# A fused FFT-mixing and ReGLU kernel: fold pieces over 26 steps, one fifth value product in 12 steps, transform work over 33 steps, tail stores per group

## Chip, cores, metric

One core of one Trainium2 chip. The metric is the device time of one execution in microseconds.

Names: PE is TensorE's matmuls, PEld its weight loads, DVE is VectorE, ACT ScalarE, POOL GpSimd, SP SyncE (which issues most transfers). An engine name with a q (SPq, ACTq, POOLq) is its sequencer, where transfers are issued.

## The reference, cut to what matters

```python
# x: (8, 3008, 256) f32; w_gate, w_val: (256, 1536); w_out: (1536, 256)
X = np.fft.fft(np.fft.fft(x, axis=1), axis=2).real      # "mixing"
gate = np.maximum(X @ w_gate, 0.0)
val  = X @ w_val
out  = gate * val @ w_out                               # (24064, 256) f32
```

## The kernel before

The sequence of 3008 is split as 94 x 32. GpSimd *folds* a batch (adds mirrored columns of x, so that half a transform is enough), TensorE runs two transform stages, and the transform along the last axis is folded into the weights. The main loop has 288 *steps*: 8 batches x 3 blocks x 12 slices `f` of the hidden width. One step makes the products for 512 rows and also for their 512 mirror rows, and it runs a twelfth of the output product of the block before. The work of the next batches (load, fold, transform) is placed at fixed steps by `plan`.

```python
# a piece of a fold; the main loop takes one piece (one yield) per step
XC = 3
def fold(b, eng):                       # eng is GpSimd
    for lo in range(1, J - 1, XC):      # XC columns at a time: 5 x 3 pieces, 2 for the ends
        ...                                                         # eo <- xl, xh (small)
        yield eng.tensor_tensor(x1[:, :, 1:D], x1[:, :, 1:D], free(xh[0:NA], ...), op=ALU.add)
        for op, o in ((ALU.add, 1), (ALU.subtract, H + 1)):
            yield eng.tensor_tensor(e1[:, :, o:o + H - 1], x1[:, :, 1:H], free(x1, ...), op=op)

def split(t):                           # which steps do without the fifth value product
    return 18 <= t < len(steps) and t % 6 != 5

# gate:  G = wc.p0 + ws.p1 -> relu -> gs  (ScalarE);  then G += wm.p1 -> relu -> gm (mirror rows)
# value: V = wc.p0, then (split) E = even part of V (VectorE), then V += ws.p1
def value(t, part):
    ...
        nc.vector.tensor_tensor(e["h"][:, 0, :], e["gs"][:], e["V"][:], op=ALU.mult)

def mirror_value(t):
    if split(t):                        # mirror value = 2*even - V on VectorE, product on GpSimd
        nc.vector.scalar_tensor_tensor(e["E"][:, cols], e["E"][:, cols], 2.0, e["V"][:, cols],
                                       op0=ALU.mult, op1=ALU.subtract)
        mirror_h(t, nc.gpsimd, e["E"])
    else:                               # unsplit: a fifth value product on TensorE, product on VectorE
        nc.tensor.matmul(e["V"][:, cols], lhsT=wm[1][...], rhs=pqt[b, blk][:, 1, cols], ...)
        mirror_h(t, nc.vector, e["V"])

# gm and E have four buffers, V three, G two (PSUM banks)

def out_piece(t, half):                 # 4 of the 96 output matmuls of a block
    ...                                 # po: one PSUM tile (one bank) for two row groups s
    if s % 2 == 1 and ff == NF - 1:
        nc.scalar.copy(os_[:, s - 1:s + 1, :], po[:])
    if s == 3 and ff == NF - 1:
        store(b, blk, sg, os_)          # four DMAs of 128 KB on SyncE's queue

# steps of load, fold, stage 1, shuffle, rotation, stage 2 of the next batches, from the batch's start
plan = {0: (18, 24, (18, 19, ...), 26, 32, (33, 34, ...)),
        1: (7, 13, range(6, 14), 14, 22, (23, 25, 27, 29, 31, 33))}
```

In an *unsplit* step TensorE does one matmul more, but VectorE does one pass less and GpSimd does no mirror product.

Of the kernel before, what the change touches and what calls it, by code (L numbers as in the profile page):

```python
# [11 lines left out]
F32 = mybir.dt.float32  # L12
# [4 lines left out]
SB = bass.MemoryType.SB  # L17
# [5 lines left out]
def view(ap, offset, dims):  # L23

    return bass.AP(ap.tensor, ap.offset + offset, [list(d) for d in dims])


def free(ap, offset, *dims):

    part = list(ap.ap[0])  # L30
    return bass.AP(ap.tensor, ap.offset + offset, [part] + [list(d) for d in dims])
# [12 lines left out]
def kernel(ctx: ExitStack, tc, x, w_gate, w_val, w_out, out):  # L44
# [3 lines left out]
    nc = tc.nc  # L48
    B, S, D = x.shape
    DF = w_gate.shape[1]  # L50
    NA, NB = 94, 32
    H = D // 2
    NF = DF // 128
    NKA = 12
    NBLK = 3
    J = NB // 2 + 1

    const = ctx.enter_context(tc.tile_pool(name="const", bufs=1, space=SB))
    xp = ctx.enter_context(tc.tile_pool(name="xp", bufs=1, space=SB))
    tp = ctx.enter_context(tc.tile_pool(name="tp", bufs=2, space=SB))  # L60
    hp = ctx.enter_context(tc.tile_pool(name="hp", bufs=2 * NF + 1, space=SB))
    psd = ctx.enter_context(tc.tile_pool(name="psd", bufs=1, space=PS))
    psg = ctx.enter_context(tc.tile_pool(name="psg", bufs=2, space=PS))
    psv = ctx.enter_context(tc.tile_pool(name="psv", bufs=3, space=PS))
# [11 lines left out]
    XC = 3  # L76

    def load_x(b, q):
        xl = xp.tile([96, J, D], F32, tag="xl", name="xl")
        xh = xp.tile([96, NB // 2, D], F32, tag="xh", name="xh")  # L80
        for p0, n in ((0, 80), (80, 14)):
            q.dma_start(out=xl[p0:p0 + n],
                        in_=view(x, b * S * D + p0 * NB * D, [[NB * D, n], [1, J * D]]))

        nc.gpsimd.indirect_dma_start(out=xh[:].rearrange("p j d -> p (j d)"), out_offset=None,
                                     in_=view(x, 0, [[NB * D // 2, 2 * B * NA], [1, NB * D // 2]]),
                                     in_offset=bass.IndirectOffsetOnAxis(ap=ix[:, b:b + 1], axis=0))
        xt[b] = (xl, xh, tp.tile([NA, J, D], BF16, tag="eo", name="eo"))

    def fold(b, eng):  # L90


        xl, xh, eo = xt[b]
        for lo in range(1, J - 1, XC):
            n = min(XC, J - 1 - lo)
            x1, e1, m = xl[0:NA, lo:lo + n, :], eo[:, lo:lo + n, :], (NB // 2 - lo) * D
            eng.tensor_tensor(free(e1, 0, [D, n], [H, 2]), free(x1, 0, [D, n], [H, 2]),
                              free(xh[0:NA], m, [-D, n], [H, 2]), op=ALU.add)
            yield eng.tensor_tensor(x1[:, :, 1:D], x1[:, :, 1:D], free(xh[0:NA], m + D - 1, [-D, n], [-1, D - 1]),  # L99
                                    op=ALU.add)  # L100
            for op, o in ((ALU.add, 1), (ALU.subtract, H + 1)):
                yield eng.tensor_tensor(e1[:, :, o:o + H - 1], x1[:, :, 1:H], free(x1, D - 1, [D, n], [-1, H - 1]),  # L102
                                        op=op)
        ends = free(xl[0:NA], 0, [(J - 1) * D, 2], [H, 2])
        eng.tensor_copy(free(eo[:], 0, [(J - 1) * D, 2], [H, 2]), ends)
        for op, o in ((ALU.add, 1), (ALU.subtract, H + 1)):
            yield eng.tensor_tensor(
                free(eo[:], o, [(J - 1) * D, 2], [1, H - 1]), free(xl[0:NA], 1, [(J - 1) * D, 2], [1, H - 1]),
                free(xl[0:NA], D - 1, [(J - 1) * D, 2], [-1, H - 1]), op=op)
# [172 lines left out]
    with tc.tile_pool(name="sp", bufs=1, space=SB) as sp:  # L282
# [124 lines left out]
        for cs, off in enumerate((o0, o1)):  # L407
# [4 lines left out]
            t2 = sp.tile([128, 4, NB], F32, tag=f"m2t{cs}")  # L412
# [26 lines left out]
        for _ in fold(1, pl):  # L439
            pass  # L440
# [9 lines left out]
    ep = ctx.enter_context(tc.tile_pool(name="ep", bufs=4, space=SB))  # L450
    op = ctx.enter_context(tc.tile_pool(name="op", bufs=2, space=SB))

    steps = [(b, blk, f) for b in range(B) for blk in range(NBLK) for f in range(NF)]
    ht = {}

    def mirrored(t):

        blk = steps[t][1]
        return slice(NB if blk == 0 else 0, 512 - NB if blk == NBLK - 1 else 512)

    def split(t):

        return 18 <= t < len(steps) and t % 6 != 5

    def gate(t):
        b, blk, f = steps[t]
# [21 lines left out]
    def value(t, part):  # L488
        b, blk, f = steps[t]
        e, pq, fs = ht[t], pqt[b, blk], slice(f * 128, (f + 1) * 128)  # L490
        if part == 0:
            e["V"] = psv.tile([128, 512], F32, tag="v", name="V")
            nc.tensor.matmul(e["V"][:], lhsT=wc[1][:, fs], rhs=pq[:, 0, :], start=True, stop=split(t))  # L493
        else:
            nc.tensor.matmul(e["V"][:], lhsT=ws[1][:, fs], rhs=pq[:, 1, :], start=False, stop=True,  # L495
                             skip_group_check=split(t))
            nc.vector.tensor_tensor(e["h"][:, 0, :], e["gs"][:], e["V"][:], op=ALU.mult)  # L497
# [8 lines left out]
    def mirror_h(t, eng, val):  # L506

        e, cols = ht[t], mirrored(t)
        eng.tensor_tensor(free(e["h"][:], 512 + cols.start + NB - 1, [NB, (cols.stop - cols.start) // NB], [-1, NB]),  # L509
                          e["gm"][:, cols].rearrange("p (a k) -> p a k", k=NB),  # L510
                          val[:, cols].rearrange("p (a k) -> p a k", k=NB), op=ALU.mult)

    def mirror_value(t):
        b, blk, f = steps[t]
        e, cols = ht[t], mirrored(t)
        if split(t):
# [3 lines that stand above are left out]
        else:  # L520
            nc.tensor.matmul(e["V"][:, cols], lhsT=wm[1][:, f * 128:(f + 1) * 128], rhs=pqt[b, blk][:, 1, cols],  # L521
                             start=False, stop=True, skip_group_check=True)
            mirror_h(t, nc.vector, e["V"])

    state = {}

    def out_piece(t, half):

        b, blk, f = steps[t]
        for k in range(8 * f + 4 * half, 8 * f + 4 * half + 4):  # L530
            gi, ff = divmod(k, NF)
            sg, s = divmod(gi, 4)
            g = 3 - s if sg else s
            if s == 0 and ff == 0:
                state["os"] = op.tile([128, 4, D], F32, tag="os", name="os")
            if s % 2 == 0 and ff == 0:
                state["po"] = pso.tile([128, 2, D], F32, tag="o", name="po")
            po, os_ = state["po"], state["os"]
            nc.tensor.matmul(po[:, s % 2, :], lhsT=ht[t - f + ff]["h"][:, sg, g * 128:(g + 1) * 128],  # L539
                             rhs=wo[:, ff, :], start=(ff == 0), stop=(ff == NF - 1))  # L540
            if s % 2 == 1 and ff == NF - 1:
                nc.scalar.copy(os_[:, s - 1:s + 1, :], po[:])  # L542
            if s == 3 and ff == NF - 1:
                store(b, blk, sg, os_)

    def store(b, blk, sg, os_):
        for u in range(4):
            ka = NKA * u + 4 * blk
            src = os_[32 * u:32 * u + 32].rearrange("p g d -> p (g d)")
            if sg == 0:  # L550
                nc.sync.dma_start(out=view(out, (b * S + ka) * D, [[NA * D, NB], [1, 4 * D]]), in_=src)
                continue

            lo = 1 if ka + 3 == 47 else 0
            hi = 3 if ka == 0 else 4
            row = b * S + NA - ka - 3 + lo
            nc.sync.dma_start(out=view(out, row * D, [[NA * D, NB], [1, (hi - lo) * D]]),
                              in_=src[:, lo * D:hi * D])
# [3 lines left out]
    def at(t, fn, *args):  # L562
        extra.setdefault(t, []).append(lambda: fn(*args))

    at(0, fold_w, 1, 1, 1, "dve")
    for k in range(4):
# [3 lines left out]


    plan = {0: (18, 24, (18, 19, 20, 21, 22, 23, 24, 25), 26, 32, (33, 34, 35, 37, 39, 41)),
            1: (7, 13, range(6, 14), 14, 22, (23, 25, 27, 29, 31, 33))}
    for b in range(B):
        t0 = b * NBLK * NF
        tl, tf, t1, tsh, tr, t2 = plan[min(b, 1)]
        if b + 2 < B:
            at(t0 + tl, load_x, b + 2, nc.sync)
            at(t0 + tf, lambda b=b: folds.append(fold(b + 2, nc.gpsimd)))
        if b + 1 < B:  # L580
            for c, k in zip((1, 2, 3, 4, 5, 6, 7, 0), t1):
                at(t0 + k, stage1, b + 1, c, "act")
            at(t0 + tsh, shuffle_out, b + 1, 0, 8)
            at(t0 + tsh, shuffle_in, b + 1, 0, NKA)
            at(t0 + tr, rotate, b + 1)
            for i, k in enumerate(t2):
                at(t0 + k, stage2, b + 1, i // 2, i % 2, "act")

    folds = []
    n = len(steps)  # L590
# [56 lines left out]
```

## Time and profile before

Median 662.8 us of 3 runs when the prediction was made. The profiled execution spans 660.6 us.

| | before |
|---|---|
| PE busy | 637.0 us (96%) |
| DVE / POOL / ACT busy | 553.3 (84%) / 468.8 (71%) / 426.7 (65%) us |
| 512-column matmuls, start to start (median) | 0.216 us |
| 256-column output matmuls, start to start (median) | 0.109 us |
| stalls of PE from step 48 on (below) | 12.7 us |
| last matmul to the end | 4.9 us |

From the page, part 1 (busy us, share of the span, number of instructions) and the first line of part 4 (the chain of work that ended last, by engine):

```profile
span 660.6 us, 12759 instructions
PE 637.0 (96%) x4266; PEld 410.1 (62%) x4266; DVE 553.3 (84%) x871; ACT 426.7 (65%) x809; POOL 468.8 (71%) x630
...
PE 81%; POOL 11%; DVE 5%; issue 2%; ACT 1%; POOLq 0%; DVEq 0%
```

TensorE is the limit almost all of the time. The 11% of GpSimd in the chain is the interesting part, since GpSimd is busy only 71% of the span.

How far a busy TensorE is from its best can be measured from the starts of its matmuls. The Trainium skill ("TensorE: Matmul & The Clock Gate", Back-to-back issue gap) gives columns/2.4 + 2.5 ns for an isolated matmul (what it says of streams is taken up in the last section), which is 215.8 ns for 512 and 109.2 ns for 256 columns; the trace's medians, 216 and 109 ns, agree. I therefore took the mirrored gate product (the trace has its record in all 288 steps), measured from one to the next, and subtracted the sum of this formula over the matmuls that the built program has between them (one small matmul of 12 columns per batch is counted as 25 ns; the traces show 29). Where nothing waits, the difference is within 6 ns of zero. The rest I call *stalls*. From step 48 to 287 the kernel has 490.7 us of matmuls and 12.7 us of stalls. They cluster in the folds: the steps from 60 to 71, for example, have 1.77 us of them, 1.13 us of it in one step, and the twelve after them 0.09 us.

GpSimd inside a fold (timeline: start us, duration us, engine, line, operation, out<-in):

```profile
162.48 0.24 POOL L97 TENSOR_TENSOR eo<-xl,xh 94x6 bf16<-94x6 f32 x1
162.79 1.81 POOL L99 TENSOR_TENSOR xl<-xl,xh 94x765 f32<-94x765 f32 x1
164.56 1.27 POOL L509 TENSOR_TENSOR h<-gm,E 128x512 bf16<-128x512 f32 x1
165.80 0.99 POOL L102 TENSOR_TENSOR eo<-xl 94x381 bf16<-94x381 f32 x1
166.74 1.27 POOL L509 TENSOR_TENSOR h<-gm,E 128x512 bf16<-128x512 f32 x1
167.98 0.99 POOL L102 TENSOR_TENSOR eo<-xl 94x381 bf16<-94x381 f32 x1
168.93 1.26 POOL L509 TENSOR_TENSOR h<-gm,E 128x512 bf16<-128x512 f32 x1
170.15 0.22 POOL L97 TENSOR_TENSOR eo<-xl,xh 94x6 bf16<-94x6 f32 x1
```

Three mirror products (L509, one per split step) and one group of three columns (L97, L99, twice L102) take 170.15 - 162.48 = 7.67 us without a gap. Three split steps of TensorE take 3 x 1.95 = 5.86 us. So during a fold GpSimd is slower than TensorE, whatever its share of the whole span. How this reaches TensorE is in the chain (start us, us, what), read from the bottom up:

```profile
156.36 1.81 POOL xl L99
158.16 1.24 POOL h L509
159.40 0.02 issue
159.42 0.02 ACT gm L486
159.45 0.47 issue
159.92 0.60 ACT gs L473
...
160.56 0.38 PE G L483
```

The mirrored gate product L483 adds into a bank that a ScalarE relu (L473) must read first, and waited for it; that relu stood behind the relu into gm (L486), which waited for a gm buffer, and the buffer was still needed by a mirror product (L509) that stood behind a 1.81 us fold piece (L99). The view of waits (engine, line, waited for: us in total, times, longest) sums these up: `ACT gm L486 <- POOL h L509: 27.4, 32, 1.4`.

```profile
ACT gm L486 <- POOL h L509: 27.4, 32, 1.4
...
DVE E L503 <- POOL h L509: 3.3, 11, 0.4
```

ScalarE's waits for PE, left out here, are healthy (it waits for work). These two lines are GpSimd holding up the engines ahead of it. What of it reaches TensorE, in the same view for TensorE alone:

```profile
PE G L483 <- ACT gs L473: 7.7, 8, 1.1
...
PE V L495 <- DVE E L503: 0.5, 3, 0.2
```

(This view covers the whole run and leaves out short waits.) Start to start and from step 48 on, 6.9 us of the 12.7 us of stalls, in 11 steps, stand before the mirrored gate product, which waits for ScalarE; 5.8 us, in 39 steps, stand before the second value product, which waits for VectorE's pass that computes E. The tail, in the timeline (a bracket gives the idle time before and what ended it):

```profile
653.16 0.58 ACT L542 COPY os<-po 128x512 f32<-128x512 f32 x1 [2.08 <-PE po L539]
655.73 0.58 ACT L542 COPY os<-po 128x512 f32<-128x512 f32 x1 [1.99 <-PE po L539]
656.34 1.72 SPq L557 DMA_DIRECT2D out_dram<-os  x4
```

After the last matmul (655.7 us) come a copy, four issues that take 1.72 us and 2.5 us until the end.

### The profile page before, as it was taken

The numbers are of one execution on the slowest core, as the hardware profiler recorded it, in microseconds if no ns is written. First come the engines' busy times: TensorE is split into PE (matmuls) and PEld (weight loads), VectorE is DVE, ScalarE is ACT, GpSimd is POOL, SyncE is SP. The second block draws the span as 40 slices with busy tenths as digits, with TensorE's granted clock in tenths as the row PEclk, the third lists the DMA queues.
The fourth block names the chain that finished last, engine by engine and source line by source line (L and its number), as shares of the span: only waits on it lengthen the run. The fifth ranks groups of instructions, "written<-read, shape, count | busy, mean of one in ns | idle before, by whom it ended". The sixth has DMA issues, their size and how long they took to land.

```text
span 660.6 us, 12759 instructions
## 1 busy us (share of the span) xinstructions
PE 637.0 (96%) x4266; PEld 410.1 (62%) x4266; DVE 553.3 (84%) x871; ACT 426.7 (65%) x809; POOL 468.8 (71%) x630
## 2 busy tenths in 40 slices
PE   6789999999999999999999999999999999999997
PEld 3424666665666666666666666666656666666665
DVE  9857688888788887989888887988979898899991
ACT  5465676775667766676676766676666766666662
POOL 9639579959975599658995599756996355455451
PEclk9799999999999999999999999999999999999999
DMA  9792472393126721196114922177111241211113
GB/s 252 239 202 51 127 202 78 85 234 104 42 78 142 192 82 49 41 196 190 40 53 106 226 81 69 51 161 221 41 42 49 67 118 39 81 33 43 51 32 94
DMA packets 32294, 70.76 MB, mean 107 GB/s; under 512 B 4475, under 2 KB 21491, under 8 KB 30227
## 3 DMA queue, kind: packets, MB, share of 16 engines
q1 hardware_dynamic: 29892, 58.16, 32.3%
q0 software_dynamic: 2336, 11.80, 9.0%
q8 instruction: 33, 0.54, 0.3%
q14 instruction: 33, 0.26, 0.1%
HBM read 39.77 MB, written 30.96 MB: 107 GB/s over the span
## 4 chain that ended last, share of the span: by engine, by line
PE 81%; POOL 11%; DVE 5%; issue 2%; ACT 1%; POOLq 0%; DVEq 0%
PE po L539 33%; PE V L495 9%; PE V L493 8%; PE G L472 8%; PE G L471 8%; PE G L483 8%; POOL h L509 3%; POOL eo L102 3%; POOL xl L99 2%; PE V L521 2%; PE ps L162 2%; POOL eo L130 2%; DVE E L503 1%; PE psw L261 1%; PE ps L204 1%
## 5 line engine op out<-in xcount | busy, mean ns | idle before, releaser
L509 POOL TENSOR_TENSOR h<-gm,E 128x480 bf16<-128x480 f32 (+1 forms) x225 | 276.0, 1227 | 147.5 <-DVE E L517 128.2
L539 PE MATMUL po<-wo,h 128*128 128x256 bf16 x2304 | 333.5, 272 | 0.0
L539 PEld LDWEIGHTS <-h 128*128 128x128 bf16 x2304 | 222.7, 98 | 88.2 <-issue 3.9
L486 ACT ACTIVATE gm<-G 128x480 f32<-128x480 f32 (+1 forms) x288 | 167.3, 581 | 141.8 <-PE G L483 112.1
L497 DVE TENSOR_TENSOR h<-gs,V 128x512 bf16<-128x512 f32 x288 | 193.9, 686 | 32.6 <-PE V L495 22.0
L503 DVE SCALAR_TENSOR_TENSOR E<-nb,af,V 128x480 f32<-128x480 bf16 (+1 forms) x225 | 163.0, 724 | 16.4 <-PE V L493 10.5
L473 ACT ACTIVATE gs<-G 128x512 f32<-128x512 f32 x288 | 171.5, 595 | 0.8 <-PE G L472 0.8
L517 DVE SCALAR_TENSOR_TENSOR E<-E,V 128x480 f32<-128x480 f32 (+1 forms) x225 | 148.1, 658 | 0.0
L483 PE MATMUL G<-pq,wm 128*128 128x480 bf16 (+1 forms) x288 | 106.6, 370 | 7.8 <-ACT gs L473 7.7
L495 PE MATMUL V<-pq,ws 128*128 128x512 bf16 x288 | 109.0, 378 | 1.1 <-DVE E L503 0.5
L472 PE MATMUL G<-pq,ws 128*128 128x512 bf16 x288 | 109.1, 379 | 0.4 <-DVE pq L209 0.4
L471 PE MATMUL G<-pq,wc 128*128 128x512 bf16 x288 | 109.1, 379 | 0.0
L493 PE MATMUL V<-pq,wc 128*128 128x512 bf16 x288 | 109.1, 379 | 0.0
L542 ACT COPY os<-po 128x512 f32<-128x512 f32 x96 | 56.2, 586 | 58.4 <-PE po L539 58.4
L509 DVE TENSOR_TENSOR h<-gm,V 128x480 bf16<-128x480 f32 (+1 forms) x63 | 41.9, 665 | 39.3 <-ACT gm L486 33.8
L102 POOL TENSOR_TENSOR eo<-xl 94x381 bf16<-94x381 f32 x70 | 69.0, 992 | 0.4
L99 POOL TENSOR_TENSOR xl<-xl,xh 94x765 f32<-94x765 f32 x35 | 63.2, 1806 | 2.7
L495 PEld LDWEIGHTS <-ws 128*128 128x128 bf16 x288 | 28.1, 98 | 33.9
L472 PEld LDWEIGHTS <-ws 128*128 128x128 bf16 x288 | 28.1, 98 | 31.5 <-issue 0.2
L172 ACT CAST t<-ps 96x512 bf16<-96x512 f32 x63 | 36.9, 585 | 6.6 <-PE ps L160 5.4
L493 PEld LDWEIGHTS <-wc 128*128 128x128 bf16 x288 | 28.1, 98 | 14.8 <-issue 7.0
L471 PEld LDWEIGHTS <-wc 128*128 128x128 bf16 x288 | 28.1, 98 | 13.1 <-issue 9.7
(106 smaller groups left out, 346.0 us busy)
## 6 DMA issues: line engine op xcount, KB each, us to landing
out_dram<-os SPq DMA_DIRECT2D x176, 128.0 KB
xl<-in_x_dram SPq DMA_DIRECT2D x7, 1360.0 KB
Td<-t SPq DMA_DIRECT2D x7, 768.0 KB
t<-Td SPq DMA_DIRECT2D x7, 768.0 KB
nb<-Nd SPq DMA_DIRECT2D x24, 128.0 KB
xl<-in_x_dram SPq DMA_DIRECT2D x7, 238.0 KB
xl<-in_x_dram SPq DMA_DIRECT2D x4, 384.0 KB
xh<-in_x_dram SPq DMA_DIRECT2D x4, 384.0 KB
```

The source lines that it names most:

```text
L471: nc.tensor.matmul(e["G"][:], lhsT=wc[0][:, fs], rhs=pq[:, 0, :], start=True, stop=False)
L472: nc.tensor.matmul(e["G"][:], lhsT=ws[0][:, fs], rhs=pq[:, 1, :], start=False, stop=True)
L473: nc.scalar.activation(e["gs"][:], e["G"][:], ACTF.Relu)
L483: nc.tensor.matmul(e["G"][:, cols], lhsT=wm[0][:, f * 128:(f + 1) * 128], rhs=pqt[b, blk][:, 1, cols], start=False, stop=True, skip_group_ ...
L486: nc.scalar.activation(e["gm"][:, cols], e["G"][:, cols], ACTF.Relu)
L493: nc.tensor.matmul(e["V"][:], lhsT=wc[1][:, fs], rhs=pq[:, 0, :], start=True, stop=split(t))
L495: nc.tensor.matmul(e["V"][:], lhsT=ws[1][:, fs], rhs=pq[:, 1, :], start=False, stop=True, skip_group_check=split(t))
L497: nc.vector.tensor_tensor(e["h"][:, 0, :], e["gs"][:], e["V"][:], op=ALU.mult)
L503: nc.vector.scalar_tensor_tensor(e["E"][:, cols], nbt[b, blk][:, cols], af[:, f:f + 1], e["V"][:, cols], op0=ALU.mult, op1=ALU.add)
L509: eng.tensor_tensor(free(e["h"][:], 512 + cols.start + NB - 1, [NB, (cols.stop - cols.start) // NB], [-1, NB]), e["gm"][:, cols].rearrange ...
L517: nc.vector.scalar_tensor_tensor(e["E"][:, cols], e["E"][:, cols], 2.0, e["V"][:, cols], op0=ALU.mult, op1=ALU.subtract)
L539: nc.tensor.matmul(po[:, s % 2, :], lhsT=ht[t - f + ff]["h"][:, sg, g * 128:(g + 1) * 128], rhs=wo[:, ff, :], start=(ff == 0), stop=(ff == ...
```

## The change

Five edits in one. The intent: fewer matmuls (20 unsplit steps become split), and to make room for what that puts on VectorE and GpSimd: smaller fold pieces over more steps, transform matmuls spread out, late mirror products moved from VectorE to ScalarE and GpSimd; and an earlier start of the last stores.

```diff
@@ fold
-        for lo in range(1, J - 1, XC):
-            n = min(XC, J - 1 - lo)
+        xc = XC if b < 3 else 2
+        for lo in range(1, J - 1, xc):
+            n = min(xc, J - 1 - lo)
@@ split
-        return 18 <= t < len(steps) and t % 6 != 5
+        return 18 <= t < len(steps) and t % (6 if t < 48 else 12) != 5
@@ mirror_value, unsplit steps
-            mirror_h(t, nc.vector, e["V"])
+            if t < 6 * NBLK * NF:
+                mirror_h(t, nc.vector, e["V"])
+            else:
+                e["E"] = ep.tile([128, 512], F32, tag="e", name="E")
+                nc.scalar.copy(e["E"][:, cols], e["V"][:, cols])
+                mirror_h(t, nc.gpsimd, e["E"])
@@ out_piece
-            if s % 2 == 1 and ff == NF - 1:
+            if ff < NF - 1:
+                continue
+            if t - f == len(steps) - NF and sg == 1:
+                nc.vector.tensor_copy(os_[:, s:s + 1, :], po[:, s % 2:s % 2 + 1, :])
+                store_last(b, blk, os_, s)
+                continue
+            if s % 2 == 1:
                 nc.scalar.copy(os_[:, s - 1:s + 1, :], po[:])
-            if s == 3 and ff == NF - 1:
+            if s == 3:
                 store(b, blk, sg, os_)
+
+    def store_last(b, blk, os_, s):
+
+        for u in range(4):
+            ka = NKA * u + 4 * blk
+            if s == 0 and ka + 3 == 47:
+                continue
+            (nc.sync if u % 2 or s < 2 else nc.scalar).dma_start(
+                out=view(out, (b * S + NA - ka - 3 + s) * D, [[NA * D, NB], [1, D]]), in_=os_[32 * u:32 * u + 32, s, :])
@@ plan
-            1: (7, 13, range(6, 14), 14, 22, (23, 25, 27, 29, 31, 33))}
+            1: (7, 13, range(6, 14), 14, 22, (23, 25, 27, 29, 31, 33)),
+            2: (7, 13, range(4, 20, 2), 20, 26, (27, 28, 30, 32, 34, 36))}
-        tl, tf, t1, tsh, tr, t2 = plan[min(b, 1)]
+        tl, tf, t1, tsh, tr, t2 = plan[min(b, 2)]
```

The main loop takes one piece of the fold per step, so pieces of two columns mean 26 pieces and 26 steps where there were 17.

More of the change, by code (lines that the diff above doesn't have):

```diff
@@ L56 @@
     J = NB // 2 + 1
+    HB = 2 * NF + 1
     const = ctx.enter_context(tc.tile_pool(name="const", bufs=1, space=SB))
@@ L60 @@
     tp = ctx.enter_context(tc.tile_pool(name="tp", bufs=2, space=SB))
-    hp = ctx.enter_context(tc.tile_pool(name="hp", bufs=2 * NF + 1, space=SB))
+    hp = ctx.enter_context(tc.tile_pool(name="hp", bufs=HB, space=SB))
     psd = ctx.enter_context(tc.tile_pool(name="psd", bufs=1, space=PS))
```

## The prediction

> **What bounds it.** TensorE: 96% busy on the page. The timeline shows 512-column matmuls starting 0.216 us apart and 256-column ones 0.108 us apart, as the Trainium skill states ("TensorE: Matmul & The Clock Gate", Back-to-back issue gap: columns/2.4 + 2.5 ns). So only fewer matmuls, fewer stalls between them, or a shorter tail can help. A "split" step has five 512-column and eight 256-column matmuls: 1.95 us. Against that spacing, start to start, the steps from 48 on hold about 15 us of stalls. They sit where GpSimd folds a batch: two steps in a fold lose about 1.0 and 1.1 us (near 155 and 172 us; later one per fold, near 250, 326, 402, 479), and many lose 0.1 to 0.3 us.
>
> **Why there.** In a fold GpSimd has no idle time (timeline, 148 to 175 us): a mirror product of 1.27 us every step, plus pieces of 0.22 + 1.80 + 2 x 0.99 us every three steps. Start to start that is about 7.5 us per three steps against TensorE's 5.86. It falls behind until the four-deep gate and value buffers are used up; then ScalarE's gate relu waits for GpSimd (waits view: gm from POOL h, 27.4 us, 32 times) and TensorE's next gate product behind it.
>
> **The change, costed.**
> 1. Twenty steps become split: 20 fifth value products fewer (13 of 480 columns, 7 of 512), 20 x 0.20 to 0.216 = -4.1 us, all on the critical path.
> 2. Five folds (batches 3 to 7) get two-column pieces. From the durations at 765, 381 and 254 elements (1.81, 0.99, 0.72 us) I estimate 2.7 us per three steps, 6.3 with the mirror products, against 5.86, less what transform matmuls and the remaining unsplit steps give back. The lag should stay under 3 us, within the buffers. About 10 us of stalls can go; I count 9.
> 3. VectorE gets 20 x (0.72 + 0.66 - 0.67) = +14 us. Start to start its split step is 1.83 us (480) to 1.90 us (512) against 1.94 and 1.95: it fits with 3% to spare, but the loop value product - even - value product is nearly as long as a step, so a delay is no longer made good soon. I count +0.7 us of new stalls. Spreading the transform matmuls gives this loop room.
> 4. From step 216 the six unsplit steps use ScalarE (0.6 us, 65% busy) and GpSimd, which has no fold then: about neutral.
> 5. Tail: now a copy (0.58), four issues (1.72) and about 2.5 us of landing. Half the copy and two issues on each of two queues: -1.3 us.
>
> Sum: -4.1 - 9 + 0.7 - 1.3 = -13.7, from 662.8: **649.0 us**, range 645.0 to 655.0. Faster by over 2% (under 649.5): 0.54; within 2%: 0.45; slower: 0.01.
>
> **What would show it.** TensorE matmuls 4266 to 4246. ScalarE's gm waiting for POOL h falls from 27 us to under 5; the 1 us stalls before the mirrored gate product vanish. VectorE's busy share rises to about 88%. Last matmul to end: 4.9 us to about 3.5. If step 2 alone fails, the gm waits stay and the time is about 657 us.
>
> **What would make it wrong.** GpSimd still outrunning its buffers because only two steps in a fold are unsplit; VectorE, its recovery steps gone, stalling TensorE by a tenth of a microsecond in many steps; the second-stage transform waiting for its shuffle (6 steps between them, not 8; the round trip took 11 us of about 12); the fold starting late because its load lands late.

## The result

Median 650.0 us (649.32 to 650.09, 4 runs) against 662.62 us (661.78 to 663.01, 4 runs). The ratio is 0.9822, 95% interval 0.9801 to 0.9842. Every ratio here is the mean time of one kernel's fast runs over that of the other kernel's fast runs of the same rounds, so it is not quite the ratio of the medians. The predicted 649.0 us with 645 to 655 was right in size (to a gain within 2%, which this is, the prediction had given 0.45, and 0.54 to a larger one); the sum is taken apart below, because one of its terms had the wrong sign.

The lines of the page that answer to those of before:

```profile
span 648.3 us, 12804 instructions
PE 626.1 (97%) x4170; PEld 408.8 (63%) x4246; DVE 565.0 (87%) x889; ACT 425.1 (66%) x813; POOL 508.1 (78%) x716
...
PE 89%; DVE 6%; issue 2%; DMA 2%; ACT 1%; SPq 0%; DVEq 0%; ACTq 0%
```

The weight loads went from 4266 to 4246, the 20 that were expected. The matmul count of 4170 is no further saving: 76 matmul records are missing from this trace, 35 of them of the first gate product alone, and the busy time of PE is a little low for the same reason. That is why stalls are measured between mirrored gate products, of which all 288 are there. GpSimd has left the chain, although it is now busy 39 us more. The line of the waits that answers to the 27.4 us of before:

```profile
ACT gm L488 <- POOL h L511: 3.4, 6, 0.6
```

And those of TensorE:

```profile
PE G L485 <- ACT gs L475: 2.2, 2, 1.1
...
PE V L497 <- DVE E L505: 1.7, 6, 0.6
```

The two waits for ScalarE lie before step 48. From there on none is left at the mirrored gate product. Of the remaining 2.3 us of stalls, 2.1 us (start to start, in 8 steps) stand before the second value product and are released by VectorE.

GpSimd in a fold, the piece of the timeline that answers to the one of before (L511 is the mirror product, L99, L101 and L104 the fold):

```profile
186.01 0.22 POOL L99 TENSOR_TENSOR eo<-xl,xh 94x4 bf16<-94x4 f32 x1
186.30 1.26 POOL L101 TENSOR_TENSOR xl<-xl,xh 94x510 f32<-94x510 f32 x1
...
187.59 1.20 POOL L511 TENSOR_TENSOR h<-gm,E 128x480 bf16<-128x480 f32 x1
188.75 0.72 POOL L104 TENSOR_TENSOR eo<-xl 94x254 bf16<-94x254 f32 x1
...
189.49 1.21 POOL L511 TENSOR_TENSOR h<-gm,E 128x480 bf16<-128x480 f32 x1
190.66 0.72 POOL L104 TENSOR_TENSOR eo<-xl 94x254 bf16<-94x254 f32 x1
...
191.40 1.20 POOL L511 TENSOR_TENSOR h<-gm,E 128x480 bf16<-128x480 f32 x1
192.57 0.20 POOL L99 TENSOR_TENSOR eo<-xl,xh 94x2 bf16<-94x2 f32 x1
```

A group of columns and three mirror products now take 192.57 - 186.01 = 6.56 us instead of 7.67 (about 0.2 us of the difference is not the change: these mirror products have 480 columns and take 1.20 us, those above have 512 and take 1.27). That is still more than TensorE's 5.86 us: GpSimd still falls behind in a fold, but slowly enough for the buffers to carry it to the next unsplit step or the end of the fold. The traces show it in the lag, from the end of VectorE's pass that makes E to the start of the mirror product that reads it: it reaches 6.3 to 6.5 us in each of the five folds of before and 3.5 to 4.9 us in those of after. The prediction had said under 3. So this is a narrow success, not a GpSimd with time to spare.

The tail:

```profile
637.44 0.42 DVE L551 COPY os<-po 128x256 f32<-128x256 f32 x1 [5.28 <-PE po L546]
637.91 2.78 PE L546 MATMUL po<-wo,h 128*128 128x256 bf16 x24 [0.57 <-DVE os L551]
638.49 7.36 SPq L565 DMA_DIRECT2D out_dram<-os  x11
...
641.19 2.83 ACTq L565 DMA_DIRECT2D out_dram<-os  x4
641.21 1.47 PE L546 MATMUL po<-wo,h 128*128 128x256 bf16 x12 [0.52 <-DVE os L551]
642.72 0.42 DVE L551 COPY os<-po 128x256 f32<-128x256 f32 x1 [1.56 <-PE po L546]
```

TensorE now waits twice (0.57 and 0.52 us) for VectorE's copies, and 11 issues of SyncE are spread over 7.36 us. From the last matmul to the end it is 5.6 us, not 4.9.

Where the 12.3 us between the two profiled executions went:

| part of the span | before | after | difference | predicted |
|---|---|---|---|---|
| start to step 48 | 141.12 | 141.01 | -0.1 | 0 |
| matmuls, steps 48 to 287 | 490.71 | 486.55 | -4.2 | -4.1 |
| stalls, steps 48 to 287 | 12.72 | 2.26 | -10.5 | -9 + 0.7 |
| last mirrored gate product to the end | 16.06 | 18.48 | +2.4 | -1.3 |
| sum | 660.6 | 648.3 | -12.3 | -13.7 |

(The first and the last row are read from the trace; the middle ones are computed as described above.)

### The profile page after: what moved, and what is told of

The parts are those of the page before. It is cut to its first block, busy times and chain, and to the rows that moved or that the text cites. A ratio compares the mean times of both kernels' runs of the same rounds, so it can differ in the third digit from the quotient of the medians.

```text
span 648.3 us, 12804 instructions
## 1 busy us (share of the span) xinstructions
PE 626.1 (97%) x4170; PEld 408.8 (63%) x4246; DVE 565.0 (87%) x889; ACT 425.1 (66%) x813; POOL 508.1 (78%) x716
## 4 chain that ended last, share of the span: by engine, by line
PE 89%; DVE 6%; issue 2%; DMA 2%; ACT 1%; SPq 0%; DVEq 0%; ACTq 0%
PE po L546 38%; PE V L497 10%; PE G L474 9%; PE G L485 9%; PE V L495 8%; PE G L473 8%; PE ps L164 2%; PE ps L206 2%; DVE E L505 2%; DVE h L499 1%; PE V L523 1%; PE psw L263 1%; DMA xl<-in_x_dram 1%; DVE eo L136 1%; DVE eo L132 1%
## 5 line engine op out<-in xcount | busy, mean ns | idle before, releaser
L511 POOL TENSOR_TENSOR h<-gm,E 128x480 bf16<-128x480 f32 (+1 forms) x251 | 307.7, 1226 | 90.9 <-DVE E L519 63.9
L505 DVE SCALAR_TENSOR_TENSOR E<-nb,af,V 128x480 f32<-128x480 bf16 (+1 forms) x245 | 177.6, 725 | 23.3 <-PE V L495 12.6
L519 DVE SCALAR_TENSOR_TENSOR E<-E,V 128x480 f32<-128x480 f32 (+1 forms) x245 | 161.2, 658 | 0.0
L495 PE MATMUL V<-pq,wc 128*128 128x512 bf16 x255 | 96.6, 379 | 0.0
L473 PE MATMUL G<-pq,wc 128*128 128x512 bf16 x253 | 95.9, 379 | 0.1
L104 POOL TENSOR_TENSOR eo<-xl 94x254 bf16<-94x254 f32 (+2 forms) x100 | 74.6, 750 | 0.4
L101 POOL TENSOR_TENSOR xl<-xl,xh 94x510 f32<-94x510 f32 (+2 forms) x50 | 65.9, 1319 | 3.9
L511 DVE TENSOR_TENSOR h<-gm,V 128x480 bf16<-128x480 f32 (+1 forms) x37 | 24.6, 665 | 22.7 <-ACT gm L488 17.1
L495 PEld LDWEIGHTS <-wc 128*128 128x128 bf16 x288 | 28.1, 98 | 11.0 <-issue 4.3
L485 PEld LDWEIGHTS <-wm 128*128 128x128 bf16 x288 | 28.2, 98 | 7.6 <-issue 4.1
```

The costliest lines, as they stand in the source:

```text
L473: nc.tensor.matmul(e["G"][:], lhsT=wc[0][:, fs], rhs=pq[:, 0, :], start=True, stop=False)
L485: nc.tensor.matmul(e["G"][:, cols], lhsT=wm[0][:, f * 128:(f + 1) * 128], rhs=pqt[b, blk][:, 1, cols], start=False, stop=True, skip_group_ ...
L495: nc.tensor.matmul(e["V"][:], lhsT=wc[1][:, fs], rhs=pq[:, 0, :], start=True, stop=split(t))
L505: nc.vector.scalar_tensor_tensor(e["E"][:, cols], nbt[b, blk][:, cols], af[:, f:f + 1], e["V"][:, cols], op0=ALU.mult, op1=ALU.add)
L511: eng.tensor_tensor(free(e["h"][:], 512 + cols.start + NB - 1, [NB, (cols.stop - cols.start) // NB], [-1, NB]), e["gm"][:, cols].rearrange ...
```

## The experiments

Twelve kernels ran, all with correct results. One more build, which gave the third fold two-column pieces too, ended in a deadlock in the simulator and did not run: such a fold is not finished when the next load takes its buffer. Each set of runs has its own runs of the kernel before beside it; *stalls* and *tail* (last mirrored gate product to the end) are from its profile. "Folds" gives the columns of a piece and the steps that a fold of batches 3 to 7 takes.

| kernel | folds | unsplit | us | ratio to before | stalls us | tail us |
|---|---|---|---|---|---|---|
| before | 3 in 17 | 1 of 6 | 662.62 | 1 | 12.7 | 16.1 |
| after | 2 in 26 | 1 of 12 | 650.00 | 0.9822 (0.9801 to 0.9842) | 2.3 | 18.5 |
| no_tail | 2 in 26 | 1 of 12 | 649.12 | 0.9803 (0.9780 to 0.9826) | 2.9 | 16.6 |
| no_fold | 3 in 17 | 1 of 12 | 670.54 | 1.0134 (1.0108 to 1.0160) | 22.0 | 18.5 |
| no_spread | 2 in 26 | 1 of 12 | 651.55 | 0.9842 (0.9812 to 0.9872) | 2.8 | 18.5 |
| no_split | 2 in 26 | 1 of 6 | 653.89 | 0.9878 (0.9856 to 0.9899) | 1.9 | 18.3 |
| fold_alone | 2 in 26 | 1 of 6 | 652.80 | 0.9869 (0.9851 to 0.9888) | 3.2 | 16.1 |
| split_alone | 3 in 17 | 1 of 12 | 666.21 | 1.0078 (1.0056 to 1.0099) | 20.2 | 16.4 |
| slow3 | 3 in 26 | 1 of 12 | 649.74 | 0.9821 (0.9803 to 0.9839) | 1.8 | 18.5 |
| fast2 | 2 in 17 | 1 of 12 | 682.71 | 1.0315 (1.0295 to 1.0335) | 34.1 | 18.5 |
| tail_sp | 2 in 26 | 1 of 12 | 649.27 | 0.9823 (0.9803 to 0.9844) | 1.9 | 18.0 |
| two_queues | 2 in 26 | 1 of 12 | 648.75 | 0.9815 (0.9792 to 0.9838) | 1.7 | 16.8 |
| pair_tail | 2 in 26 | 1 of 12 | 647.65 | 0.9793 (0.9772 to 0.9814) | 1.4 | 15.7 |
| no_mirror | 2 in 26 | 1 of 12 | 650.78, one run | not timed | 2.5 | 18.5 |

The tail is the most repeatable part: after and the five other kernels with its tail and its last step (no_fold, no_spread, slow3, fast2, no_mirror) have 18.47 or 18.48 us. The time from the start to step 48, which none of these edits touches, is 140.5 to 142.8 us in these profiles. That and stalls of 0.3 to 0.8 us that come and go are the scatter behind the times, so small differences are judged by the parts of the trace.

### Undo one part of the change

**no_tail**: the change without the branch for the last block.

```diff
-            if t - f == len(steps) - NF and sg == 1:
-                nc.vector.tensor_copy(os_[:, s:s + 1, :], po[:, s % 2:s % 2 + 1, :])
-                store_last(b, blk, os_, s)
-                continue
```

> The change without its tail: the last block is copied in pairs by ScalarE and stored four rows at a time from one queue, as before. Theory: the new tail costs time. In the profile of after, TensorE waits twice (0.57 and 0.52 us) for VectorE's copies of the shared output bank, and SyncE's fifth small store waits about 2.4 us for a completion semaphore that a later ScalarE store had taken first, so the end comes 18.5 us after the last mirrored gate product, against 16.1 us in before. Without it: 2.0 to 2.4 us less than after, about 647.8 us, and from the last matmul to the end 4.9 us again. Rival (my prediction): the tail saves 1.3 us, so this run is slower than after, about 651.3 us.

Measured: the tail is 16.58 us, 1.90 less than after's 18.48, so the new tail costs time, and the rival (my prediction) falls. The whole run gained only 0.9 us in the median, less than expected, and its trace has 0.65 us more stalls elsewhere (0.69 us in step 134, which no other kernel with folds of 26 steps has). The 1.90 us are 1.40 before the last matmul (VectorE's copies: start to start, the two waits in after's trace cost 0.73 and 0.68 us) and 0.49 after it.

**no_fold**: three-column pieces, everything else changed.

```diff
-        xc = XC if b < 3 else 2
+        xc = XC
```

> The change with all folds in three-column pieces (17 steps), the rest as changed. Theory: long GpSimd pieces are what made the 1 us stalls, and with only one or two unsplit steps in a fold GpSimd falls further behind than before: at least 1.4 us per fold of stalls back in five folds, 7 to 12 us more than after, about 657 to 662 us, with ScalarE's gm waiting for GpSimd 25 us or more. Rival: the clustered transform work of the old plan made the stalls; then this stays within 2 us of after.

Measured: 670.54 us, 20.5 us more than after and slower even than the kernel before. The direction was right, the size was twice what I expected. Its view of waits:

```profile
DVE E L505 <- POOL h L511: 18.1, 32, 1.4
ACT gm L488 <- POOL h L511: 17.1, 27, 1.2
...
PE V L497 <- DVE E L505: 12.5, 14, 1.4
```

GpSimd holds up VectorE (no free E buffer) as much as ScalarE (no free gm buffer), together 35.2 us against 30.7 us in the kernel before. Both cost TensorE time, VectorE the more: start to start, 18.8 us of the stalls stand before the second value product and 3.1 us before the mirrored gate product. In each fold two or three steps lose 1.1 to 1.4 us.

**no_spread**: the old transform steps.

```diff
-        tl, tf, t1, tsh, tr, t2 = plan[min(b, 2)]
+        tl, tf, t1, tsh, tr, t2 = plan[min(b, 1)]
```

> The change with the old transform steps for batches 2 and on, the rest as changed. Theory: the folds are the main cause, the spreading only gives VectorE room at steps after an unsplit one: 1.5 to 4 us more than after, about 652 to 654 us, as stalls of 0.1 to 0.3 us before the second value product. Rival (clustering made the 1 us stalls): 7 us or more, 657 us or more, with 1 us stalls back.

Measured: 651.55 us, 1.55 more, just within what I expected, but only 0.5 us of it are stalls (2.76 against 2.26 us): 0.11 and 0.06 us in the step after each unsplit one, as before the change. Of the rest, the larger part is the start of this execution: the profile reaches step 48 1.36 us later than after's, and the first mirrored gate product is already 1.86 us later (38.62 against 36.76 us), although nothing there differs. So the spreading is worth about half a microsecond, and clustered transform work was not the cause of the 1 us stalls.

**no_split**: the fifth value product in 1 of 6 steps, on VectorE.

```diff
-        return 18 <= t < len(steps) and t % (6 if t < 48 else 12) != 5
+        return 18 <= t < len(steps) and t % 6 != 5
-            if t < 6 * NBLK * NF:
+            if True:
```

> The change with the fifth value product in 1 of 6 steps throughout, on VectorE, the rest as changed: 20 matmuls more (4225 in the build against 4205). Theory: TensorE has no slack, so 20 x 0.20 to 0.216 = 4.1 us more, plus up to 1.5 us of 0.06 to 0.11 us stalls after the unsplit steps: about 654 to 655.7 us. Rival: with fewer unsplit steps VectorE and GpSimd lose their recovery and gave back part of the gain; then this is less than 3 us slower than after.

Measured: 653.89 us, 3.9 more than after, with 4.16 us more matmuls and about the same stalls (1.92 us). The 20 matmuls are worth their full time, once GpSimd is not in the way. (The built programs have 4242 and 4222 matmul instructions, not the 4225 and 4205 named above; the difference is 20 either way.)

### Do one part alone

**fold_alone**: the kernel before with `xc = XC if b < 3 else 2` in the fold. **split_alone**: the kernel before with `t % (6 if t < 48 else 12) != 5` in `split`.

> The kernel before with only the two-column folds of batches 3 to 7. Theory: it takes the 1 us stalls away and most of the 0.1 to 0.3 us ones in the folds, of 12.7 us of stalls from step 48 on some 8 to 9 us: ratio to before 0.986 to 0.989, about 653 to 655 us. Rival (the gain needs the spread transform work too): less than 4 us gained.

> The kernel before with only the rule 1 of 12 for the fifth value product. Theory: TensorE does 4.1 us less, but every unsplit step that a fold loses is a mirror product more for GpSimd, which is the limit inside a fold; the stalls grow by more than the matmuls save: 4 to 10 us slower than before, about 667 to 672 us. Rival (TensorE is the limit everywhere): about 4 us faster than before.

Measured: fold_alone 652.80 us (ratio 0.9869), stalls from 12.7 down to 3.2 us. split_alone 666.21 us (ratio 1.0078): 4.16 us of matmuls saved, 7.5 us of stalls added. It is slower than its runs of the kernel before by 4.6 us (666.21 against 661.65), at the lower end of the 4 to 10 us that I expected. So the two parts are not two gains that add up: alone, removing TensorE's work makes the kernel slower; after the fold is spread, it is worth 4 us.

### Length of a piece, or rate of the work?

The change does both at once: smaller pieces and fewer columns per step. The main loop was edited to separate them. **slow3** has three-column pieces and leaves out every third step; **fast2** has two-column pieces and takes two in every odd step.

```diff
-        while folds and next(folds[0], folds) is folds:
-            folds.pop(0)
+        for _ in range(0 if t >= 48 and t % 3 == 2 else 1):     # slow3, with xc = XC
+        for _ in range(2 if t >= 48 and t % 2 else 1):          # fast2
+            while folds and next(folds[0], folds) is folds:
+                folds.pop(0)
```

> The change with three-column pieces as in the kernel before, but one piece in two of every three steps, so that a fold takes 26 steps too. It tells the length of a piece from the rate of the work. Theory (rate: GpSimd falls behind by total work per step): within 2.5 us of after, 648 to 652.5 us. Rival (the 1.8 us piece itself blocks the mirror products): 656 us or more, half or more of the 20 us that three-column pieces in 17 steps cost.

> The change with its two-column pieces, but three pieces in every two steps, so that a fold takes 17 to 18 steps as before. Theory (rate): as bad as three-column pieces in 17 steps or a little worse, since small pieces have more fixed cost: 668 to 676 us. Rival (length of a piece): within 2.5 us of after.

Measured: slow3 649.74 us and 1.8 us of stalls, the same as after. fast2 682.71 us and 34.1 us of stalls, the worst kernel of all, and worse than the 668 to 676 us that I expected. Its view of waits:

```profile
ACT gm L488 <- POOL h L511: 42.6, 38, 2.5
DVE E L505 <- POOL h L511: 27.5, 19, 1.6
```

The length of a piece does not matter here (1.8 us pieces stand in the way of mirror products in slow3 just as before); the work per step does. Smaller pieces even cost more in total, since each GpSimd instruction has a fixed part: 765, 381 and 254 elements took 1.81, 0.99 and 0.72 us, which fits 2.13 ns per element and 0.18 us each. The five folds together occupy GpSimd for 113 us (after) and 115 us (fast2) in pieces of two columns, and for 104 us (before, no_fold, slow3) in pieces of three; that may be most of the 12 us of stalls that fast2 has above no_fold, though no run separates it from the two pieces that fast2 puts into one step. The slope agrees with the Trainium skill ("GPSIMD Engine Reference", Elementwise: 4497 ns for an addition of 2048 fp32 elements, which I estimate from it at about 2.2 ns each).

### The tail

**tail_sp**: all 15 small stores on SyncE's queue.

```diff
-            (nc.sync if u % 2 or s < 2 else nc.scalar).dma_start(
+            nc.sync.dma_start(
```

> The change with all 15 small stores of the last half block issued by SyncE (four of them were ScalarE's). In the build the stores now take the eight completion semaphores in their own order. Theory (in after SyncE's fifth small store stood 2.4 us waiting for a completion semaphore that a later ScalarE store had taken): that wait is gone although one queue now issues everything; 15 issues of 0.43 us end about 645.2 us instead of 645.85, so from the last mirrored gate product to the end 17.8 us against after's 18.5, no_tail's 16.6 and before's 16.1. The two waits of TensorE on VectorE's copies (0.57 and 0.52 us) stay. Rival (one queue is simply the limit, two queues are better): longer than 18.5 us, since 4 more issues of 0.43 us stand in one queue.

Measured: the tail is 17.99 us instead of 18.48, and the 15 issues end 2.69 us after the last matmul instead of the 11 of SyncE 3.17 us after it. The view of SyncE's own waits for after's last 12 us has this line, and tail_sp's has none for these stores:

```profile
SPq L565 <- DMA out_dram<-os: 2.4, 1, 2.4
```

What it waited for is read from the built programs: stores use eight completion semaphores in turn. In after the turn was given out with ScalarE's stores of the third group ahead of SyncE's of the second, so SyncE's next store of the second group had to wait until a store of ScalarE that comes 1.3 us later in the data's order had landed. One queue was faster than two, so the rival falls, in the trace: the times, with ratios to before of 0.9823 and 0.9822, don't show half a microsecond. The two waits of TensorE for copies are there in tail_sp too (0.57 and 0.52 us): they belong to the copies, not to the stores. A copy per group reads half of a bank while the next group's matmuls want to write the other half. The Trainium skill ("PSUM — Partial Sum Buffer", PSUM bank collisions raise a hardware error) says that two engines must not touch the same bank in the same 32 partitions at the same time, even at different addresses; both use all 128 partitions here, so this wait cannot be dropped, only avoided by copying pairs or by giving each group a bank of its own.

**two_queues**: the tail of before, the last four stores alternately on two queues.

```diff
+            last = (b, blk) == (B - 1, NBLK - 1)
-            nc.sync.dma_start(out=view(out, row * D, ...
+            (nc.scalar if last and u % 2 else nc.sync).dma_start(out=view(out, row * D, ...
```

> The change with the tail of before, except that the last four stores go alternately through SyncE and ScalarE. Theory: what can be had at the tail is the issue of two of four stores, 2 x 0.43 us: 15.7 us from the last mirrored gate product to the end against no_tail's 16.6, and in time about 2.7 us less than after, some 647.3 us. Rival: ScalarE's queue is no faster or collides with the other; then 16.6 us or more.

Measured: no gain. The timeline shows the issues side by side:

```profile
641.83 0.78 SPq L576 DMA_DIRECT2D out_dram<-os  x2
641.84 0.86 ACTq L576 DMA_DIRECT2D out_dram<-os  x2
```

The last issue ended 1.51 us after the last matmul instead of 2.36, but the last packet of data ended 3.57 us after it, as in no_tail (3.59). The four stores are 0.49 MB, and between their first and last packet 2.1 us pass, 0.23 MB per us: the end is bound by the data, not by the issuing. The Trainium skill says as much ("DMA: Bandwidth & Descriptors", Issuing engines are not separate DMA queues: more issuing engines only save the sequencer's time). My theory for this run was wrong. (The tail is even 0.2 us longer than no_tail's. Both end with an instruction fetch of 0.53 us in the closing barrier that before and after do not have.)

**pair_tail**: half of these bytes moved forward. Pairs are copied by ScalarE as before, and each pair of the last half block is stored at once.

```diff
+            if t - f == len(steps) - NF and sg == 1:
+                if s % 2 == 1:
+                    store_pair(b, blk, os_, s - 1)     # two rows; the last pair alternately on two queues
+            elif s == 3:
                 store(b, blk, sg, os_)
```

> The version meant to beat both kernels: as two_queues, and the first pair of rows of the last half block is stored as soon as it is copied, so the last four stores carry 2 KB per row instead of 4. TensorE waits for no copy, since pairs leave the output bank together. Theory: the landing of the last stores shortens by up to 0.4 us: 15.3 to 15.7 us from the last mirrored gate product to the end, 646.6 to 647.3 us in time, ratio to before 0.977 to 0.978. Rival: the landing does not depend on the size; then equal to two_queues.

Measured: tail 15.72 us, 0.86 less than no_tail and 2.76 less than after; the last data ended 2.67 us after the last matmul, 0.92 us earlier than in two_queues. 647.65 us, ratio 0.9793 (0.9772 to 0.9814): the fastest kernel here, though a little short of what I expected in time, and its interval overlaps those of no_tail and two_queues. Its advantage over after in the tail of the trace is clear; in the times it is 2.35 us between medians of different rounds.

**no_mirror**: the late unsplit steps' mirror products left on VectorE (`if True:` in `mirror_value`).

> The change with the mirror product of the six late unsplit steps (from step 216 on) left on VectorE. Theory: VectorE is then late for the next step and TensorE loses 0.06 to 0.12 us in the step after each, as in the kernel before: at most 0.5 us in all, to be seen in the trace, not in the time. Rival: VectorE would hold TensorE up by a microsecond or more in the last two batches.

Measured: stalls in the last three blocks are 0.38, 0.18 and 0.38 us instead of 0.26, 0 and 0: at most 0.7 us in all (VectorE late by 0.06 to 0.32 us in the steps concerned). A small gain, as expected, slightly above the 0.5 us I gave it.

## Why the prediction was right, and where it was not

**What bounds the kernel** was right: TensorE, and GpSimd inside the folds. The formula for the spacing reproduces the steps to a few nanoseconds. The way from GpSimd to TensorE was told only in part: beside ScalarE's gate relu there is a second one, over VectorE's pass that computes E, and no_fold loses most of its time there.

**Point 1, twenty matmuls, -4.1 us**: measured -4.16 us in the trace, and no_split lost 3.9 us in time. "All on the critical path" was true only because of point 2: split_alone had the same 20 matmuls fewer and was slower than before.

**Point 2, the folds, -9 us**: right in mechanism, and nearly in size: the fold alone took the stalls from 12.7 to 3.2 us (fold_alone), and together with the other points it was -10.5 us. The estimate of 6.3 us per three steps was 6.56 in the trace, and the lag of under 3 us was 3.5 to 4.9. The prediction named two-column pieces as the cause; what counts is the rate. slow3 reaches the same with three-column pieces, fast2 with two-column pieces in 17 steps loses 33 us to after. "If step 2 alone fails ... about 657 us" was far too small: no_fold is 670.5 us. I had only put back the stalls of before, and had not reckoned that every unsplit step taken away is a mirror product more for an engine that is already behind.

**Point 3, VectorE, +0.7 us of new stalls**: right in kind, but on balance too small to be seen. VectorE's busy share rose from 84% to 87% (predicted 88%). New stalls did come where the prediction put them, before the second value product: 0.34, 0.27 and 0.26 us in steps 157, 183 and 262 of after, each released by VectorE's pass that computes E, and in none of the kernels with the 1 of 6 rule (before, fold_alone, no_split). In exchange, most stalls of 0.06 to 0.11 us after unsplit steps went with those steps. The sum is 2.3 us in after against 1.9 in no_split, and among the five kernels with after's main loop (after, no_tail, tail_sp, two_queues, pair_tail) it scatters from 1.4 to 2.9. That spreading the transform matmuls gives it room is true and small: 0.5 us (no_spread).

**Point 4, neutral**: right, at most 0.7 us in its favour (no_mirror).

**Point 5, the tail, "half the copy and two issues on each of two queues: -1.3 us"**: this is the step that failed. The tail grew by 2.4 us. I counted only what follows the last matmul and took it to be bound by issuing. The runs show four things in its place: TensorE waits for the copies of a shared bank (no_tail: 1.40 us before the last matmul); SyncE stood 2.4 us behind a semaphore taken by a later store (tail_sp: 0.5 us of it reached the end); even with free queues the end is bound by data (two_queues); and the last step, unsplit before, is split now and makes TensorE wait for VectorE before its second value product, 0.3 us (the last matmul ends 11.46 us after the start of the last mirrored gate product in no_tail and split_alone, 11.15 in before and fold_alone). The other 0.2 us of the 2.4 follow the last matmul and were not traced.

The two errors, +3.7 us in the tail and -2.2 us in the stalls, partly cancelled: that 649.0 came so near to 650.0 is luck.

**What stays open.** Some stalls recur at fixed places of a program (0.35 us in step 54 of every kernel; those in steps 157, 183 and 262 in after and most of its variants; one of 0.33 us in step 211 in before, fold_alone and no_split). In all of them TensorE waits for VectorE. In after, VectorE had itself stood idle for 0.32 to 0.36 us just before the stalls of steps 157, 183 and 262; what it waited for there was not settled. They cost about 1 us.

## What to carry to other kernels

An engine that is 71% busy over the span can be the limit in the stretch where extra work is dealt out to it: compare its work per step with the step's length there, and when it is too much, spread the work over more steps; the size of the pieces is secondary. Before a matmul is traded for work on other engines, see whether one of them is the limit at that place: here the same trade cost 4.6 us alone and gained 4 us after the spreading. At a kernel's end, look at three things apart: whether the copies hold up the last matmuls, whether the issues wait for each other's semaphores, and how many bytes are left to move.

## What the Trainium skill lacked or had wrong

- "TensorE: Matmul & The Clock Gate", Back-to-back issue gap: it calls the formula that held here that of an isolated matmul, and gives a sustained spacing of about 131 ns for 512 columns in a stream of weight load and matmul pairs. This kernel is such a stream and shows 216 ns (median), in the main loop never less than 215; for 256 columns 109 ns.
- No page that I read says that stores share eight completion semaphores in turn, as they do in these built programs, and that the turn can run against the order of the data: 2.4 us of SyncE's time in after, none in tail_sp.
- "DMA: Bandwidth & Descriptors", Issuing engines are not separate DMA queues: right, but it calls the issuing usually small relative to the transfer. Here four issues of SyncE take 1.72 us and their 0.49 MB 2.1 us.
- "Perfetto Trace Analysis" does not warn that records can be missing: 76 of 4246 matmuls in the trace of after, none in that of before, which would read as a saving of 96 matmuls where it was 20.
